# Attention and a gated feed-forward layer in one planned program: due times of the first two units found by trials, scores over 232 keys, and a planned lag before transposes and values

## The chip, the cores and the metric

The kernel runs on one core of one Trainium2 chip. What counts is the device time of one execution in microseconds (us). The engines are TensorE (PE, with its weight loads shown apart as PEld), VectorE (DVE), ScalarE (ACT), GpSimd (POOL) and SyncE (SP, which issues the DMAs here). Each runs its own instructions in a fixed order, and they wait for one another by semaphores.

## What is computed

Sliding-window attention with some global keys, for 4 batches, 8 heads, 768 positions and a head size of 64, and then a gated feed-forward layer over all 3072 tokens (model size 512, inner size 1536). The calls have `n_global` = 8 and `n_local` = 96.

```python
scores = scale * np.matmul(q, k.transpose(0, 1, 3, 2))
is_global = pos[None, :] < int(n_global)
is_local = (rel >= 0) & (rel < int(n_local))
keep = is_global | is_local
dist = np.where(is_global & ~is_local, float(n_local), np.abs(rel))
scores = np.where(keep, scores - slopes * dist, -1000000000.0)
a = softmax(scores)
x = np.matmul(a, v)            # heads side by side: 512 columns per token
out = ((x @ w_a) * (x @ w_b)) @ w_out
```

A query block of 128 positions therefore needs its own 128 keys, the 96 before them and the first 8 of the sequence: 232 keys. The weights arrive as 64-bit floats.

## The kernel before

**Units.** The 24 query blocks (4 batches of 6) are cut into eight units of 4, 2, 3, 3, 3, 3, 3 and 3 blocks (`UNITS`). For a unit, attention makes x, and `moe` runs the feed-forward layer on its tokens in 12 groups `f` of 128 inner columns. Attention of unit u+1 is meant to lie beside the feed-forward layer of unit u; attention of unit 0 (`first`) stands alone at the start. Units 0 and 1 (`PAIRED`) do two heads at once in fp32 (`quad`, scores on L673); units 2 to 7 split q and k into a high and a low fp32r part (`split`) and make each window of scores of two matmuls (`scores` in `attention`, L793).

**Windows.** `Plan` lists for each block which keys it sees. With `G` = 32 and `LW` = 96 a block sees 32 + 96 + 128 = 256 keys. The first block of a batch has 128, and the second shares the first one's keys (joined: 256). `kwin` is the place and width of a block's window of keys, and `vslot` the slots of 128 rows of V that go with it.

**One window.** The scores go to PSUM (`ps`). DVE adds the distance mask and takes the extreme (L537), ACT takes the exponential with its sum (L553), DVE makes the inverse of the sum (L568, L575), ACT or DVE normalises (L585, L587). PE transposes the 128-column pieces (`turn`, L609), ACT or DVE copies them out of PSUM (`pf`, L341 or L343), and PE multiplies them with V (`values`, L626). The mask `rel` and its narrow form `col` are built once, before the first unit (`build_positions`, `build_masks`).

**Feed-forward layer.** For each f, two projections (`p`, L851) of 4 chunks with 3 matmuls each (high and low parts), their product on DVE (L890), its split in two (`hh`, `hl`), and the product with `w_out` into one PSUM bank per block (`acc`, L869). The weights of the 12 groups are converted from 64-bit once, beside unit 0's layer (`load_w`): per half group ACT runs L381 and L418, DVE runs L388, L398, L408, L427 and L351, and one cast (`wt`) runs on ACT (L341) or DVE (L343).

**The order.** Each step is an `Op` with a due time, what it reads and writes, and a cost on each engine that may run it. `Schedule.order` simulates the engines with these costs and with lags between engines (`LAGS`). An engine that comes free takes, among the steps whose inputs are there and whose buffers fit, the one that is due first; `wins` chooses between engines. The order so found is the order in which the instructions are written out. Steps of the first unit have due times before `START` = 52000 (ns), and the layer of unit u is due in equal steps from there.

Of the kernel before, what the change touches and what calls it, by code (L numbers as in the profile page):

```python
# [3 lines left out]

# [8 lines left out]
F32 = mybir.dt.float32  # L13
# [11 lines left out]
P = 128  # L25
# [4 lines left out]
NT = B * S  # L30
G = 32
LW = 96
# [11 lines left out]
SLACK = 1.5  # L44
BACKLOG = 1.0
PRICE = {"dve": 2.0, "pool": 2.0}
TRACE = False
LAGS = {"pe": 200.0, "act": 270.0, "dve": 230.0, "pool": 290.0, "dma": 2300.0}
# [12 lines left out]
class Plan:  # L61
# [4 lines left out]
    def __init__(self, blocks, paired):  # L66
        self.nb = len(blocks)
        self.kkeys = []
        self.vkeys = []
        self.kwin = []  # L70
        self.vslot = []
        self.parts = []
        for n, (b, blk) in enumerate(blocks):
            if blk == 0:
                keys = np.arange(P)
            else:
                q0 = blk * P
                keys = np.concatenate([np.arange(G), np.arange(q0 - LW, q0 + P)])
# [3 lines left out]
            if joined:  # L82
                self.kwin.append((self.kwin[-1][0], 2 * P))
                self.kkeys += [(b, j) for j in keys[P:]]
                self.vslot.append([self.vslot[-1][0], len(self.vkeys)])
                self.vkeys.append((b, keys[P:]))
            else:
                self.kwin.append((len(self.kkeys), len(keys)))
                self.kkeys += [(b, j) for j in keys]
                slots = []  # L90
                for c in range(len(keys) // P):
                    slots.append(len(self.vkeys))
                    self.vkeys.append((b, keys[c * P : (c + 1) * P]))
                self.vslot.append(slots)
        self.nk = len(self.kkeys)
        self.nv = len(self.vkeys)
        self.k0 = self.nb * P
        self.ncol = self.k0 + self.nk // 2
        if paired:

            ends = self.parts[1:] + [self.nk]
            self.pieces = []
            at = 0
            for k, end in zip(self.parts, ends):
                self.pieces.append((at, at + 2 * P - k, 2 * P + end - k, (k, end)))
                at += 2 * P + end - k
            self.ncol = at
# [43 lines left out]
class Op:  # L151
    def __init__(self, index, due, costs, emit, reads, writes, late, port):
        self.index, self.due, self.costs, self.emit, self.late = index, due, costs, emit, late
        self.port = port
        self.bufs, self.after, self.before = [], [], 0
        self.ready, self.engine = 0.0, None
        found = {}
        for is_write, keys in ((False, reads), (True, writes)):
            for key in keys:
                buf, part = key if isinstance(key, tuple) else (key, None)  # L160
                if buf not in self.bufs:
                    self.bufs.append(buf)
                for other, p, w in buf.log:
                    if (w or is_write) and other is not self and (p == part or p is None or part is None):
                        found[other.index] = other
                buf.log.append((self, part, is_write))
        for other in found.values():
            other.after.append(self)
            self.before += 1
        for buf in self.bufs:  # L170
            buf.left += 1


class Schedule:
# [13 lines left out]

    def op(self, due, emit, reads=(), writes=(), late=0.0, port=(), **costs):

        self.ops.append(Op(len(self.ops), due, costs, emit, reads, writes, late, port))

    def order(self):
        free = {e: 0.0 for e in self.SYNC}
# [9 lines left out]
        def arrive(op):  # L204
            for e in op.costs:
                insort(ready[e], (op.due, op.index, op))

# [9 lines left out]
        def wins(op, e):  # L217
            if len(op.costs) == 1:
                return True
            at = {}  # L220
            for o, c in op.costs.items():
                at[o] = max(free[o], now) + c * PRICE.get(o, 1.0)
                for due, index, other in ready[o]:
                    if (due, index) >= (op.due, op.index):
# [5 lines left out]
        for op in self.ops:  # L230
            if not op.before:
                arrive(op)
        while len(out) < len(self.ops):
            started = True
# [31 lines left out]
            if kind == 0:  # L266
                for nxt in op.after:
                    if op.engine == "pe" and tuple(nxt.costs) == ("pe",):
# [37 lines left out]
class Fast:  # L306
# [52 lines left out]
    def load_w(self, f, due):  # L359
# [3 lines left out]
        for g in range(2):  # L363
# [19 lines left out]
                [st],  # L383
                act=act(WN) + 40,
            )
# [36 lines left out]
                [(raw, "lo")],  # L422
                act=act(WN) + 40,
            )
# [105 lines left out]
    def softmax(self, h, due, wins, ps, t, sm):  # L530

        nc, op, n = self.nc, self.plan.op, len(wins)
        for j, (o, w) in enumerate(wins):
            neg = self.negd if w == 2 * P else self.negd0
            op(
# [65 lines left out]

    def turn(self, due, wins, t, pt, pf):

        nc = self.nc
        w = sum(w for o, w in wins)

        def emit(e):
            for c in range(0, w, P):
                nc.tensor.transpose(pt[:, c : c + P], t[:, c : c + P], self.ident)  # L609

        self.plan.op(due, emit, [t], [pt], pe=w / P * 109)
        self.copy(due, lambda: pf[:, :w], lambda: pt[:, :w], w, [pt], [pf], psum=True)

    def values(self, due, pl, blocks, v, probs, pa):
# [20 lines left out]
        n = sum(len(pl.vslot[i]) for i in blocks)  # L635
        self.plan.op(due, emit, reads, [pa], pe=n * 218 + 200)

    def quad(self, u, c, j, due, raw, v, pa, homes):
# [44 lines left out]
        for s in range(2):  # L683
# [11 lines left out]
            self.turn(due, wins, t, pt, pf)  # L695
            for i, (o, w) in zip(blocks, wins):
                probs[s, i] = (pf, o)
        if pa is None:
            pa = self.bank("psS", f"pa{n}")
# [68 lines left out]
    def attention(self, u, start, end):  # L768
# [8 lines left out]
        for c in range(NCC):  # L777
            probs = {}
            v = self.fetch_v(u, c, start + (2 * c + 1) * step - LOADLEAD)
            for s in range(2):  # L780
# [4 lines left out]
                for i in range(pl.nb):  # L785
# [143 lines left out]
    def run(self):  # L929
# [238 lines left out]
def build_positions(nc, cp, tp):  # L1168


    rel = cp.tile([P, 2 * P], F32, name="rel")
    col = cp.tile([P, P], F32, name="col")
    for t, step, base, mult in ((rel, -1, P, 1), (col, 1, 0, 0)):
        nc.gpsimd.iota(
# [5 lines left out]
        )  # L1180
    t = tp.tile([P, 2 * P], F32, name="after")
    nc.vector.tensor_scalar(t, rel, 0.0, BIG, op0=ALU.is_lt, op1=ALU.mult)
    nc.vector.tensor_tensor(rel, rel, t, op=ALU.max)
    return rel, col, t


def build_masks(nc, rel, col, t, nf):

    v, ng, nl = nc.vector, nf[:, 0:1], nf[:, 1:2]
    v.tensor_scalar(t, rel, nl, -BIG, op0=ALU.is_ge, op1=ALU.mult)
    v.tensor_scalar(col, col, ng, -BIG, op0=ALU.is_ge, op1=ALU.mult)
    v.tensor_sub(rel, t, rel)
    v.tensor_scalar(col, col, nl, None, op0=ALU.subtract)
    v.tensor_copy(rel[:, :G], col[:, :G])
    v.tensor_tensor(col, rel[:, P:], col, op=ALU.max)

# [23 lines left out]
def build(nc, a, out):  # L1222
    with tile.TileContext(nc) as tc, ExitStack() as ctx:
        cp = ctx.enter_context(tc.tile_pool(name="c", bufs=1))
        with tc.manual_schedule(), tc.tile_pool(name="tmp", bufs=1) as tp:
# [4 lines left out]
            nc.scalar.activation(spare, lim[:, 0:1], AF.Exp)  # L1230
            rel, col, t = build_positions(nc, cp, tp)
            sc = build_scales(nc, cp)
# [4 lines left out]
            flag = build_flag(nc, cp, nf, lim)  # L1237
            build_masks(nc, rel, col, t, nf)
        fast = nc.values_load(flag[0:1, 0:1], min_val=0, max_val=2**30)
# [12 lines left out]
def pack(q, k, v):  # L1252
# [6 lines left out]
    for u, (blocks, pl) in enumerate(zip(UNITS, PLANS)):  # L1259
# [21 lines left out]
        for c in range(NCC):  # L1281
            vs = [v[b, 2 * c + s, keys] for s in range(2) for b, keys in pl.vkeys]
            put(VOFFS[u][c], np.hstack(vs))
# [32 lines left out]
```

## Time and profile before

| | us |
|---|---|
| median of 3 runs (777.14 to 778.99) | 778.75 |
| the profiled execution | 777.36 |
| its span, first to last instruction | 775.1 |
| PE busy | 751.5 |
| PEld busy | 663.6 |
| DVE busy | 438.7 |
| ACT busy | 433.7 |

PE is busy for 97% of the span, but a matmul's record overlaps the next one's, so a busy PE is not yet a PE at its peak; what a matmul costs in a dense stretch is seen from start to start. DVE and ACT are busy for 57% and 56% of the span on average, and far more at the beginning. The granted TensorE clock was 0.995 of full speed on average.

### The profile page before, as it was taken

Reading aid. Unit: us, or ns where it says so; the run is one execution under the profiler, and the core shown is the slowest. Engines: PE = TensorE matmul, PEld = TensorE weight load, DVE = VectorE, ACT = ScalarE, POOL = GpSimd, SP = SyncE. Lnnn points to the kernel's source line nnn. Section 1 sums busy time; section 2 is a strip of 40 time slices with the busy share of each in tenths; the row PEclk is TensorE's granted clock in tenths of the full one; section 3 lists DMA queues with packets and bytes.
Section 4 is the critical chain, followed back from the end, with each engine's and each line's share of the span. In section 5 each row is a group of like instructions: output and inputs, shape, how many; then the busy total and the mean of one; then the engine's idle time right before and its main releaser. Section 6 shows DMA issues by size and latency. Waiting matters only on the chain.

```text
span 775.1 us, 12558 instructions
## 1 busy us (share of the span) xinstructions
PE 751.5 (97%) x4608; PEld 663.6 (86%) x4608; DVE 438.7 (57%) x1375; ACT 433.7 (56%) x1093; POOL 6.6 (1%) x24
## 2 busy tenths in 40 slices
PE   5799999999999999999999999999999999999997
PEld 4567777798998998989988988999988999889996
DVE  6999999766655654445554554455554545522111
ACT  6999756466656556455555565555544655442111
POOL 1000000000000000000000000000000000000000
PEclk9999999999999999999999999999999999999999
DMA  7888101032221111211112111111112121000001
GB/s 287 334 321 340 35 14 31 32 107 65 75 90 41 62 38 49 72 48 49 43 54 89 42 62 48 48 60 48 52 42 62 62 62 41 0 28 15 1 1 45
DMA packets 20086, 58.04 MB, mean 75 GB/s; under 512 B 2352, under 2 KB 2608, under 8 KB 20016
## 3 DMA queue, kind: packets, MB, share of 16 engines
q1 hardware_dynamic: 20016, 57.16, 21.5%
q8 instruction: 38, 0.62, 0.3%
q14 instruction: 32, 0.26, 0.1%
HBM read 50.86 MB, written 6.29 MB: 74 GB/s over the span
## 4 chain that ended last, share of the span: by engine, by line
PE 84%; DVE 7%; ACT 6%; issue 1%; DMA 1%; ACTq 0%; DVEq 0%
PE p L851 45%; PE acc L869 23%; PE pt L609 5%; PE pa L626 5%; PE ps L793 4%; PE ps L673 1%; ACT wr L418 1%; DVE kk L351 1%; DVE t L537 1%; ACT t L553 1%; ACT t L585 1%; ACT wm L381 1%; DVE wm L408 1%; ACT pf L341 1%; DVE wt L351 1%
## 5 line engine op out<-in xcount | busy, mean ns | idle before, releaser
L851 PE MATMUL p<-xh,wt 128*128 128x384 f32 (+2 forms) x1488 | 438.9, 345 | 4.0 <-DVE wt L343 2.3
L851 PEld LDWEIGHTS p<-xh,wt 128*128 128x128 f32 x1488 | 272.9, 189 | 18.2 <-issue 3.6
L851 PE MATMUL p<-xl,wt 128*128 128x384 f32 (+2 forms) x816 | 269.8, 342 | 0.2 <-DVE xl L351 0.2
L869 PE MATMUL acc<-wt,hh 128*128 128x512 f32 x576 | 206.4, 397 | 0.0
L851 PEld LDWEIGHTS p<-xl,wt 128*128 128x128 f32 x816 | 153.8, 189 | 10.3 <-DVE xl L351 1.4
L890 DVE TENSOR_TENSOR raw<-p,raw 128x384 f32<-128x384 f32 (+2 forms) x96 | 53.4, 557 | 153.5 <-PE p L851 146.8
L869 PEld LDWEIGHTS acc<-wt,hh 128*128 128x128 f32 x576 | 108.3, 188 | 19.0 <-issue 0.5
L553 ACT ACTIVATE t<-t,sm 128x256 f32<-128x256 f32 (+1 forms) x192 | 93.8, 491 | 40.0 <-DVE sm L537 39.0
L869 PE MATMUL acc<-wt,hl 128*128 128x512 f32 x288 | 113.0, 392 | 0.0
L585 ACT ACTIVATE t<-t,sm 128x256 f32<-128x256 f32 (+1 forms) x140 | 68.7, 494 | 71.1 <-DVE sm L575 66.2
L537 DVE CUSTOM_DVE_ANT_0 t<-ps,rel 128x256 f32<-128x256 f32 x160 | 66.6, 421 | 66.9 <-PE ps L793 64.4
L341 ACT COPY raw<-p 128x384 f32<-128x384 f32 (+2 forms) x95 | 45.3, 477 | 70.7 <-PE p L851 70.1
L609 PE MATMUL pt<-ident,t 128*128 128x128 f32 x352 | 68.6, 280 | 5.3 <-ACT t L585 2.5
L341 ACT COPY pf<-pt 128x256 f32<-128x256 f32 (+3 forms) x151 | 56.2, 375 | 22.6 <-PE pt L609 21.6
L351 DVE TENSOR_TENSOR hl<-raw,hh 128x384 fp32r<-128x384 f32 (+2 forms) x96 | 53.4, 556 | 23.7 <-ACT hh L341 23.1
L609 PEld LDWEIGHTS pt<-ident,t 128*128 128x128 f32 x352 | 43.2, 140 | 25.5 <-ACT t L585 10.1
L341 ACT CAST hh<-raw 128x384 fp32r<-128x384 f32 (+2 forms) x85 | 43.6, 513 | 35.9 <-DVE raw L890 34.9
L869 PEld LDWEIGHTS acc<-wt,hl 128*128 128x128 f32 x288 | 54.2, 188 | 6.6
L568 DVE TENSOR_SCALAR sm<-sm 128x1 f32<-128x1 f32 (+1 forms) x168 | 25.7, 153 | 43.5 <-ACT t L553 42.4
L351 DVE TENSOR_TENSOR kk<-raw,kk 64x384 fp32r<-64x384 f32 (+1 forms) x90 | 44.2, 491 | 2.8
L626 PE MATMUL pa<-pf,v 128*64 128x128 f32 x640 | 42.8, 278 | 2.4 <-ACT pf L341 1.9
L626 PEld LDWEIGHTS pa<-pf,v 128*64 128x64 f32 x640 | 34.7, 136 | 11.6 <-issue 5.0
(78 smaller groups left out, 604.7 us busy)
## 6 DMA issues: line engine op xcount, KB each, us to landing
wr<-wts SPq DMA_DIRECT2D x24, 768.0 KB, 12.5
raw<-qkv SPq DMA_DIRECT2D x29, 384.0 KB, 3.0
raw<-qkv SPq DMA_DIRECT2D x24, 320.0 KB, 2.9
v<-qkv SPq DMA_DIRECT2D x16, 384.0 KB, 3.1
out<-o SPq DMA_DIRECT2D x23, 256.0 KB, 2.1
v<-qkv SPq DMA_DIRECT2D x16, 256.0 KB, 2.7
raw<-qkv SPq DMA_DIRECT2D x3, 640.0 KB, 6.0
raw<-qkv SPq DMA_DIRECT2D x1, 256.0 KB, 3.5
```

Source lines behind the costliest of these rows:

```text
L341: self.nc.scalar.copy(out(), src())
L351: lambda e: self.engine(e).tensor_sub(out(), a(), b()),
L537: lambda e, j=j, o=o, w=w, neg=neg: nc.vector.tensor_tensor_reduce(t[:, o : o + w], ps[:, o : o + w], neg[:, :w], -(2.0 ** -(h + 1)), 3.0e ...
L553: lambda e, j=j, o=o, w=w: nc.scalar.activation(t[:, o : o + w], t[:, o : o + w], AF.Exp, bias=sm[:, j : j + 1], scale=-1.0, accum_out=sm[ ...
L568: lambda e: nc.vector.tensor_scalar_add(sm[:, 2 * n : 3 * n], sm[:, n : 2 * n], 1e-9),
L585: nc.scalar.mul(t[:, o : o + w], t[:, o : o + w], r)
L609: nc.tensor.transpose(pt[:, c : c + P], t[:, c : c + P], self.ident)
L626: nc.tensor.matmul(pa[D * s : D * s + D, i * P : i * P + P], v[:, v0 : v0 + D], pf[:, o + c * P : o + c * P + P], start=c == 0, stop=c == ...
L793: nc.tensor.matmul(ps[:, :w], q[:, i * P : i * P + P], kk[:, k0 : k0 + w], start=m == 0, stop=m == 1,)
L851: nc.tensor.matmul(p[:, :T], wt(), b[:, b0 : b0 + T], start=c == 0 and n == 0, stop=c == NCC - 1 and n == 2,)
L869: nc.tensor.matmul(acc[i][:, :], hs[:, i * P : i * P + P], wt(), start=f == 0 and n == 0, stop=f == NF - 1 and n == 2,)
L890: lambda e, asb=asb, pb=pb: nc.vector.tensor_mul(asb[:, :T], pb[:, :T], asb[:, :T]),
```

## The change

**Fewer keys.** `G` goes from 32 to 8, so that a window is 128 + 96 + 8 = 232 keys wide. The order of the keys is turned round: own block, the 96 before, the global ones. The second transpose of a 232 window takes columns 104 to 231; its first 24 columns are there a second time, so the V slot that goes with it has 24 rows of zeros ahead of its 104 keys. The masks are built in the new order, from three index fills in place of two. Joined windows stay at 256 and first blocks at 128.

**A planned lag.** Steps have a field `spare` in place of `late`: the time by which the planner lets a step come later than its input plus the lag. Transposes and values of units 2 to 7 get `SPARE` = 200 ns. The planner's costs change too: transposes 112 ns each in place of 109, values +290 in place of +200, the two ACT steps of the weight conversion +72 in place of +40.

**A search.** `Schedule.search` takes the steps that are due before the end of the second unit's layer, plans them with `order`, and then tries 400 times to move the due time of about 3 in 100 of them at random (normal, 4000 ns). A trial that ends earlier by the model is kept. At last the whole program is planned with the due times so found.

```diff
-G = 32
+G = 8
...
+SPARE = 200.0
...
+TRIES = 400
+SHARE = 0.03
+SPREAD = 4000.0
...
-            joined = blk == 1 and n > 0
...
+            head = np.concatenate([np.arange(P - LW, P), np.arange(P - LW)])
+            if blk == 0:
+                own = np.arange(P, 2 * P) if (b, 1) in blocks else np.arange(0)
+                self.kwin.append((at + len(own), P))
+                self.kkeys += [(b, j) for j in own] + [(b, j) for j in head]
+                self.vslot.append([slot])
+                self.vkeys.append((b, head))
+            elif blk == 1 and n:
+                start, _ = self.kwin[-1]
+                self.kwin.append((start - P, 2 * P))
+                self.vslot.append([slot, self.vslot[-1][0]])
+                self.vkeys.append((b, np.arange(P, 2 * P)))
             else:
...
+                keys = np.concatenate([np.arange(q0, q0 + P), np.arange(q0 - LW, q0), np.arange(G)])
+                self.kwin.append((at, len(keys)))
...
+                self.vkeys += [(b, keys[:P]), (b, keys[P:])]
...
+    def search(self, limit, tries, share, spread):
+        rnd = random.Random(1)
+        ops = [op for op in self.ops if op.due < limit]
+        dues = {op.index: op.due for op in ops}
+        best = self.order(ops, dues)[1]
+        for _ in range(tries):
+            trial = dict(dues)
+            for op in ops:
+                if rnd.random() < share:
+                    trial[op.index] += rnd.gauss(0.0, spread)
+            end = self.order(ops, trial)[1]
+            if end < best:
+                best, dues = end, trial
+        return self.order(self.ops, {op.index: dues.get(op.index, op.due) for op in self.ops})
...
-                        lag = self.SYNC[op.engine] + op.late
+                        lag = self.SYNC[op.engine] + nxt.spare
...
-                act=act(WN) + 40,
+                act=act(WN) + 72,
...
-    def turn(self, due, wins, t, pt, pf):
+    def turn(self, due, wins, t, pt, pf, spare=0.0):
...
+        starts = []
+        for o, w in wins:
+            starts += [o] if w == P else [o, o + w - P]
+        n = len(starts) * P
...
-        self.plan.op(due, emit, [t], [pt], pe=w / P * 109)
-        self.copy(due, lambda: pf[:, :w], lambda: pt[:, :w], w, [pt], [pf], psum=True)
+                nc.tensor.transpose(pt[:, c * P : c * P + P], t[:, o : o + P], self.ident)
+        self.plan.op(due, emit, [t], [pt], pe=len(starts) * 112, spare=spare)
+        self.copy(due, lambda: pf[:, :n], lambda: pt[:, :n], n, [pt], [pf], psum=True)
...
-        self.plan.op(due, emit, reads, [pa], pe=n * 218 + 200)
+        self.plan.op(due, emit, reads, [pa], pe=n * 218 + 290, spare=SPARE if pl.late else 0.0)
...
-                    self.turn(due, [(0, w)], t, pt, pf)
+                    self.turn(due, [(0, w)], t, pt, pf, SPARE)
...
+        t2 = t + NF * (steps[0] + steps[1])
...
-        order, end = self.plan.order()
+        order, end = self.plan.search(t2, TRIES, SHARE, SPREAD)
...
+    for t, base, step, mult in (
+        (rel[:, :P], 0, -1, 1),
+        (rel[:, P:], LW, -1, 1),
+        (first, 0, 1, 0),
+    ):
...
+            vs = [
+                np.vstack([np.zeros((P - len(keys), D), q.dtype), v[b, 2 * c + s, keys]])
+                for s in range(2)
+                for b, keys in pl.vkeys
+            ]
```

More of the change, by code (lines that the diff above doesn't have):

```diff
@@ L3 @@
 from heapq import heappop, heappush
+import random
 import numpy as np
@@ L67, in __init__ @@
         self.nb = len(blocks)
+        self.late = not paired
         self.kkeys = []
@@ L73, in __init__ @@
         for n, (b, blk) in enumerate(blocks):
[L74 to L78, printed above, removed]
-            joined = blk == 1 and n > 0
             if paired and n % 2 == 0:
                 self.parts.append(len(self.kkeys))
[L82 to L86, printed above, removed]
-            else:
-                self.kwin.append((len(self.kkeys), len(keys)))
+            at, slot, q0 = len(self.kkeys), len(self.vkeys), blk * P
+            head = np.concatenate([np.arange(P - LW, P), np.arange(P - LW)])
[10 more added lines that the diff above has]
+                self.vkeys.append((b, np.arange(P, 2 * P)))
+            else:
+                keys = np.concatenate([np.arange(q0, q0 + P), np.arange(q0 - LW, q0), np.arange(G)])
+                self.kwin.append((at, len(keys)))
                 self.kkeys += [(b, j) for j in keys]
[L90 to L94, printed above, removed]
+                self.vslot.append([slot, slot + 1])
+                self.vkeys += [(b, keys[:P]), (b, keys[P:])]
         self.nk = len(self.kkeys)
@@ L151, with __init__ @@
 class Op:
-    def __init__(self, index, due, costs, emit, reads, writes, late, port):
-        self.index, self.due, self.costs, self.emit, self.late = index, due, costs, emit, late
+    def __init__(self, index, due, costs, emit, reads, writes, spare, port):
+        self.index, self.due, self.costs, self.emit, self.spare = index, due, costs, emit, spare
         self.port = port
@@ L171, in __init__, with fresh @@
             buf.left += 1
+        self.found = list(found.values())
+    def fresh(self, due, ops):
+        self.at, self.ready, self.engine = due, 0.0, None
+        self.before = sum(other.index in ops for other in self.found)
+        for buf in self.bufs:
+            buf.left = 0
 class Schedule:
@@ L187, in buf, with op, order @@
         return b
-    def op(self, due, emit, reads=(), writes=(), late=0.0, port=(), **costs):
-        self.ops.append(Op(len(self.ops), due, costs, emit, reads, writes, late, port))
-    def order(self):
+    def op(self, due, emit, reads=(), writes=(), spare=0.0, port=(), **costs):
+        self.ops.append(Op(len(self.ops), due, costs, emit, reads, writes, spare, port))
+    def search(self, limit, tries, share, spread):
[12 more added lines that the diff above has]
+        return self.order(self.ops, {op.index: dues.get(op.index, op.due) for op in self.ops})
+    def order(self, ops, dues):
+        for op in ops:
+            op.fresh(dues[op.index], dues)
+        for op in ops:
+            for buf in op.bufs:
+                buf.left += 1
         free = {e: 0.0 for e in self.SYNC}
@@ L205, in arrive @@
             for e in op.costs:
-                insort(ready[e], (op.due, op.index, op))
+                insort(ready[e], (op.at, op.index, op))
         def fits(op):
@@ L223, in wins @@
                 for due, index, other in ready[o]:
-                    if (due, index) >= (op.due, op.index):
+                    if (due, index) >= (op.at, op.index):
                         break
@@ L228, in wins @@
             return at[e] <= min(at.values()) + 40.0
-        for op in self.ops:
+        for op in ops:
             if not op.before:
                 arrive(op)
-        while len(out) < len(self.ops):
+        while len(out) < len(ops):
             started = True
@@ L267, in order @@
                 for nxt in op.after:
+                    if nxt.index not in dues:
+                        continue
                     if op.engine == "pe" and tuple(nxt.costs) == ("pe",):
@@ L422, in load_w @@
                 [(raw, "lo")],
-                act=act(WN) + 40,
+                act=act(WN) + 72,
             )
@@ L533, in softmax @@
         for j, (o, w) in enumerate(wins):
-            neg = self.negd if w == 2 * P else self.negd0
+            neg = self.negd if w > P else self.negd0
             op(
@@ L600, in softmax @@
             )
-    def turn(self, due, wins, t, pt, pf):
+    def turn(self, due, wins, t, pt, pf, spare=0.0):
         nc = self.nc
-        w = sum(w for o, w in wins)
+        starts = []
+        for o, w in wins:
+            starts += [o] if w == P else [o, o + w - P]
+        n = len(starts) * P
         def emit(e):
-            for c in range(0, w, P):
-                nc.tensor.transpose(pt[:, c : c + P], t[:, c : c + P], self.ident)
-        self.plan.op(due, emit, [t], [pt], pe=w / P * 109)
-        self.copy(due, lambda: pf[:, :w], lambda: pt[:, :w], w, [pt], [pf], psum=True)
+            for c, o in enumerate(starts):
+                nc.tensor.transpose(pt[:, c * P : c * P + P], t[:, o : o + P], self.ident)
+        self.plan.op(due, emit, [t], [pt], pe=len(starts) * 112, spare=spare)
+        self.copy(due, lambda: pf[:, :n], lambda: pt[:, :n], n, [pt], [pf], psum=True)
     def values(self, due, pl, blocks, v, probs, pa):
@@ L695, in quad @@
             self.turn(due, wins, t, pt, pf)
-            for i, (o, w) in zip(blocks, wins):
+            o = 0
+            for i in blocks:
                 probs[s, i] = (pf, o)
+                o += len(pl.vslot[i]) * P
         if pa is None:
@@ L1172, in build_positions @@
     col = cp.tile([P, P], F32, name="col")
-    for t, step, base, mult in ((rel, -1, P, 1), (col, 1, 0, 0)):
+    first = tp.tile([P, P - LW], F32, name="first")
+    for t, base, step, mult in (
[3 more added lines that the diff above has]
+    ):
         nc.gpsimd.iota(
@@ L1180, in build_positions, with build_masks @@
         )
[L1181 to L1187, printed above, removed]
-    v, ng, nl = nc.vector, nf[:, 0:1], nf[:, 1:2]
[L1192 to L1197, printed above, removed]
+    t = tp.tile([P, P + LW], F32, name="after")
+    nc.vector.tensor_scalar(t[:, :P], rel[:, :P], 0.0, BIG, op0=ALU.is_lt, op1=ALU.mult)
+    nc.vector.tensor_tensor(rel[:, :P], rel[:, :P], t[:, :P], op=ALU.max)
+    return rel, col, first, t
+def build_masks(nc, rel, col, first, t, nf):
+    v, ng, nl = nc.vector, nf[:, 0:1], nf[:, 1:2]
+    n = P + LW
+    v.tensor_scalar(t, rel[:, :n], nl, -BIG, op0=ALU.is_ge, op1=ALU.mult)
+    v.tensor_scalar(first, first, ng, -BIG, op0=ALU.is_ge, op1=ALU.mult)
+    v.tensor_sub(rel[:, :n], t, rel[:, :n])
+    v.tensor_scalar(rel[:, n:], first, nl, None, op0=ALU.subtract)
+    v.tensor_copy(col[:, :LW], rel[:, P - LW : P])
+    v.tensor_tensor(col[:, LW:], rel[:, : P - LW], rel[:, n:], op=ALU.max)
 def build_scales(nc, cp):
@@ L1230, in build @@
             nc.scalar.activation(spare, lim[:, 0:1], AF.Exp)
-            rel, col, t = build_positions(nc, cp, tp)
+            rel, col, first, t = build_positions(nc, cp, tp)
             sc = build_scales(nc, cp)
@@ L1237, in build @@
             flag = build_flag(nc, cp, nf, lim)
-            build_masks(nc, rel, col, t, nf)
+            build_masks(nc, rel, col, first, t, nf)
         fast = nc.values_load(flag[0:1, 0:1], min_val=0, max_val=2**30)
@@ L1281, in pack @@
         for c in range(NCC):
-            vs = [v[b, 2 * c + s, keys] for s in range(2) for b, keys in pl.vkeys]
+            vs = [
[3 more added lines that the diff above has]
+            ]
             put(VOFFS[u][c], np.hstack(vs))
```

## The prediction, made before the changed kernel was run

> **What bounds the kernel now.** I read the busy table first (it stands above), then the same table by stages, then the chain of work in order of time, then the waits of TensorE (PE) and the groups of instructions. The stages (length, then busy time of PE, PEld, DVE, ACT, POOL, granted clock, DMA):
>
> ```profile
> 7.60:20.00 12.40, 10.40 (x76) 7.08 (x75) 9.86 (x60) 10.23 (x37) 0.00 (x0) 0.86 1.02 403
> 20.00:32.00 12.00, 10.54 (x102) 7.33 (x100) 10.97 (x63) 12.00 (x43) 0.00 (x0) 1.00 0.95 390
> 32.00:40.00 8.00, 3.28 (x33) 2.22 (x29) 7.42 (x13) 8.00 (x19) 0.00 (x0) 0.97 0.69 261
> 40.00:45.00 5.00, 5.00 (x20) 4.10 (x21) 5.00 (x14) 5.00 (x9) 0.00 (x0) 0.70 0.85 348
> 45.00:80.00 35.00, 34.12 (x174) 26.32 (x174) 34.36 (x62) 34.85 (x58) 0.00 (x0) 1.00 0.77 303
> 80.00:140.00 60.00, 59.62 (x293) 46.87 (x292) 59.29 (x108) 37.58 (x67) 0.00 (x0) 1.00 0.09 25
> ...
> 160.00:700.00 540.00, 537.41 (x3443) 487.52 (x3442) 282.23 (x988) 301.18 (x816) 4.40 (x6) 1.00 0.18 55
> ```
>
> PE is the bound from about 40 us on. From 160 to 700 us it is busy 537.41 of 540, with VectorE (DVE) and ScalarE (ACT) near half. Before 40 us, ACT has no idle time from 20 us on, and DVE hardly any; PE waits for them. From 40 to 140 us PE and DVE are both full: DVE converts the weights while PE uses them, with attention of the second unit as PE's filler. So a gain is to be had in three places: fewer PE cycles anywhere after 40 us, fewer PE stalls after 160 us, and an earlier and smoother first 140 us.
>
> **The change part by part.**
>
> Scores over 232 keys. What a matmul of fp32r costs when PE is dense is read from start to start in the chain (start, length, what, count):
>
> ```profile
> 127.82 5.60 PE p L851 x24
> ...
> 198.38 1.39 PE p L851 x12
> 199.77 0.23 PE ps L793 x2
> ...
> 711.42 4.16 PE p L851 x24
> ...
> 197.58 0.17 PE ps L793 x2
> ```
>
> The L851 rows are 512, 256 and 384 columns wide (the units of four, two and three blocks): 5.60/24 = 233 ns, 1.39/12 = 116 ns, 4.16/24 = 173 ns. That is (173 - 116)/128 = 0.445 ns a column, so 24 columns fewer are 10.7 ns. The scores of the late units follow it: 0.23 us for two of 256 columns. The first block of a batch stays at 128 and the second at 256 (its window joins the first), so per head each batch has four windows of 232. In units 2 to 7 that is 3 x 8 + 9 x 8 = 96 windows of two matmuls: 192 x 10.7 ns = 2.05 us. The pair of 128 columns takes 0.17, not the 0.12 that the slope gives, so something floors narrow matmuls; drawn from 0.17 to 0.23 the slope gives only 96 x 11 ns = 1.1 us. 232 lies next to 256, where the steeper slope holds, so **-2.0 us**, between -1.1 and -2.05. PE is full there, so it counts in full. In the first two units the scores (L673) lie where PE is not alone the bound; I count nothing for them on PE.
>
> Transposes and values keep their number: each 232 window still has two transposes (the second starts at column 104) and two value slots, padded with 24 zero rows, so the copies out of PSUM and the V loads stay as they are. Query/key loads and key splits of the late units get 24 columns a window shorter, on engines half idle: nothing there.
>
> The planned lag. This adds no instruction and no wait: it makes the planner place each transpose and each values step of units 2 to 7 at least 0.2 us after its input, so that other PE work goes first. What it can remove is seen from 160 to 700 us in the waits of PE and of its weight loads:
>
> ```profile
> PE pt L609 <- ACT t L585: 1.9, 7, 0.5
> ...
> PE p L851 <- DVE xl L351: 0.2, 1, 0.2
> ...
> PEld pt L609 <- ACT t L585: 8.8, 23, 0.8
> ```
>
> and in one of these waits, the longest, in the timeline:
>
> ```profile
> 290.32 0.34 PE L851 MATMUL p<-xh,wt 128*128 128x384 f32 x1
> ...
> 291.16 0.20 PEld L609 LDWEIGHTS pt<-ident,t 128*128 128x128 f32 x2 [0.82 <-ACT t L585]
> 291.16 0.44 PE L609 MATMUL pt<-ident,t 128*128 128x128 f32 x2 [0.50 <-ACT t L585]
> ```
>
> A projection matmul starts at 290.32 and another could start 0.173 us later, at 290.49; the transpose starts at 291.16. The stall is 0.67 us. PE's own idle time shows 0.50 of it, because the record of a matmul reaches into the next; the weight loads show 0.82, 0.15 too much. Over 23 waits: 8.8 - 23 x 0.15 = 5.35 us really stalled (estimate). A lag of 0.2 us takes at most 23 x 0.2 = 4.6 us off them, and nothing off what is shorter than that. I take **-3.5 us**; ends 0 (the fixed order meets as many other late inputs) and -5.35. What is queued behind a later transpose: ACT's copy of it, the values, the x copies and the split before the next unit's first projection. That last wait is 0.2 us in all now, and the code ends each attention 1.5 of 12 weight groups early, so 0.2 us a step is covered; if that cover were gone, each of the six unit borders would cost one lag or two, 6 x 0.4 = 2.4 us.
>
> Narrower work in the first 140 us. Per window of 232 instead of 256:
>
> ```profile
> L553 ACT ACTIVATE t<-t,sm 128x256 f32<-128x256 f32 x160 | 81.1, 509 | 35.2 <-DVE sm L537 34.7
> L537 DVE CUSTOM_DVE_ANT_0 t<-ps,rel 128x256 f32<-128x256 f32 x160 | 66.6, 421 | 66.9 <-PE ps L793 64.4 <-PE pt L609 0.8 <-PE ps L673 0.4
> ...
> L587 DVE TENSOR_SCALAR t<-t,sm 128x256 f32<-128x256 f32 x41 | 13.9, 350 | 0.6
> ...
> L553 ACT ACTIVATE t<-t,sm 128x128 f32<-128x128 f32 x32 | 12.8, 401 | 4.8 <-DVE sm L537 4.3
> L537 DVE CUSTOM_DVE_ANT_0 t<-ps,col 128x128 f32<-128x128 f32 x32 | 9.1, 283 | 7.2 <-PE ps L793 5.0 <-PE ps L673 2.2
> ...
> L587 DVE TENSOR_SCALAR t<-t,sm 128x128 f32<-128x128 f32 x11 | 3.1, 284 | 0.2
> ```
>
> DVE: (421 - 283)/128 x 24 = 26 ns, and 12 ns where it normalises, (350 - 284)/128 x 24. ACT: (509 - 401)/128 x 24 = 20 ns. Units 0 and 1 have two such windows each for 8 heads, 32 in all: DVE 32 x 26 + 16 x 12 = 1.0 us, ACT 0.65 us. DVE is full there, so **-0.8 us**, between 0 (if it only makes another hole) and -1.0.
>
> The new mask set-up: three POOL index fills in place of two, and the same six DVE steps on fewer columns. The first score step of DVE waits 1.0 us for PE:
>
> ```profile
> 7.60 0.29 DVE L537 CUSTOM_DVE_ANT_0 t<-ps,col 128x128 f32<-128x128 f32 x1 [1.00 <-PE ps L673]
> ```
>
> This hides it: nothing. Without that cover one more fill would be 0.2 to 0.3 us.
>
> The searched plan. 400 trials change the order of all engines in the first two units, the DMA issues on SP's queue too, and keep what the planner's model says ends first. How much is there? DVE's idle time from 7.6 to 140 us is 2.54 + 1.03 + 0.58 + 0 + 0.64 + 0.71 = 5.5 us by the stage rows; ACT's is 2.17 up to 45 us and 0.15 to 80, but 22.4 from 80 to 140. The DVE work itself does not go: in 40 to 140 us it is mostly
>
> ```profile
> L408 DVE SCALAR_TENSOR_TENSOR wm<-wr,wm 128x768 int32<-128x768 int32 x22 | 20.6, 949 | 0.0
> L427 DVE CUSTOM_DVE_ANT_0 wm<-wr,wm 128x1536 uint16<-128x1536 uint16 x22 | 20.6, 948 | 0.0
> L351 DVE TENSOR_TENSOR wt<-wm,wt 128x768 fp32r<-128x768 f32 x21 | 19.9, 951 | 0.3 <-ACT wt L341 0.3
> L388 DVE TENSOR_SCALAR wm<-wm 128x768 f32<-128x768 f32 x22 | 11.8, 552 | 0.0
> L398 DVE TENSOR_SCALAR wm<-wm 128x768 int32<-128x768 int32 x22 | 11.8, 552 | 0.0
> ```
>
> 84.7 us of weight conversion that only DVE does in this program. Loads are shaken with the rest, and a weight load takes
>
> ```profile
> wr<-wts SPq DMA_DIRECT2D x24, 768.0 KB, 12.5
> ```
>
> from issue to landing (KB, us), with DMA at 0.69 to 1.02 up to 45 us; but no row of ACT's waits names these loads, so a shift by a few us stays covered by their lead. So a perfect order gains about 5.5 us, a useless one 0. Does a gain in the model carry over? The planner's costs against spacings in the chain:
>
> ```profile
> 32.01 0.80 ACT wm L381
> 32.81 0.83 ACT wr L418
> ...
> 36.28 0.87 DVE wm L427
> ```
>
> The ACT conversion is put at 93 + 0.833 x 768 + 72 = 805 ns in the new text (773 before), the DVE step at 67 + 1.045 x 768 = 870 ns: close. I take about a third of 5.5, **-1.7 us**, since every trial keeps a plan fitted to the model alone and lags between engines are single numbers in it. The dearer values (+90 ns) and transposes (+3 ns each) only make the plan place them better; they are within the lag's term.
>
> Sum: -2.0 - 3.5 - 0.8 - 1.7 = -8.0 us. The profiled execution took 777.36 (span 775.1 and 2.3 around it): 769.4. It lies 1.4 under the median of 778.75, which would give 770.75. I predict **770.0**, between them.
>
> **The rivals.**
>
> (All from 778.0, the middle of 777.36 and 778.75.) Only what is certain: the lag moves the stalls elsewhere and the search finds a model's gain alone. For it: 5.35 us of stalls lie in 23 places, and a fixed order can meet 23 others; against it: the close costs above. Scores and narrower windows stay: 778 - 2.8 = 775.2.
>
> The search closes DVE's holes and the lag takes its 4.6: 778 - 2.0 - 4.6 - 1.0 - 5.5 = 764.9. For it: ACT's 22 us of idle time, to which work that either engine can do may move; against it: holes at the start have inputs that are late for everyone.
>
> The clock. After PE's waits of 2.3 and 1.0 us the first projections run slow:
>
> ```profile
> PE p L851 <- DVE wt L343: 2.3, 1, 2.3
> ...
> PE p L851 <- DVE wt L351: 1.0, 1, 1.0
> ...
> 39.87 4.01 PE p L851 x10
> ```
>
> 401 ns each instead of 233, at a granted clock of 0.70 from 40 to 45 us: 10 x 168 ns = 1.7 us. If the new order keeps PE at work before its first projections, this goes on top of the forecast: 768.3. Against it: DVE supplies the weights then, and PE might only wait where it now runs slowly. The Trainium skill, TensorE: Matmul & The Clock Gate, Part 1, says that an idle window of about 3.4 us puts the clock back to half, in windows that run freely; the trace agrees, with 2.3 + 1.0 us of waits ahead of the slow matmuls.
>
> Slower: weight casts go over to DVE. Three of the 24 casts that either engine can do run on DVE now:
>
> ```profile
> L343 DVE CAST wt<-wm 128x768 fp32r<-128x768 f32 x3 | 1.7, 553 | 0.0
> ```
>
> With ACT's conversions priced 32 ns dearer and due times shaken at random, the planner could hand it the other 21: 21 x 0.553 = 11.6 us on the engine that is full from 40 to 140 us. With the scores and the lag kept: 778 - 2.0 - 3.5 + 11.6 = 784.1. It decides from 5.5/0.553, about 10 casts moved on. Against it: the planner counts DVE time double when it chooses.
>
> **How the numbers follow.** A measurement of this kernel tells about 0.3% from no change, 2.3 us: faster means under 776.4, slower over 781.1. Forecast (766 to 773.5) 0.56; only the certain part (773.5 to 777.5) 0.18; holes closed 0.10; clock 0.07; casts on DVE 0.09. Two thirds of the second case lie under 776.4, so faster is 0.56 + 0.12 + 0.10 + 0.07 = 0.85; the rest of it and a third of the last, where few casts move, give same 0.09; slower 0.06. The range from 763.0 to 776.5 leaves out the last case, the worst of the second, and what lies beyond the best.
>
> **What would show it right or wrong.** Now the first projection, and the span of the last weight steps, stand so:
>
> ```profile
> 38.14 0.50 PE L851 MATMUL p<-xh,wt 128*128 128x512 f32 x1 [2.33 <-DVE wt L343]
> ...
> L351 DVE TENSOR_TENSOR wt<-wm,wt x24: 943/951/960, 38.9 to 143.6; 128x768 fp32r<-128x768 f32 x24
> ```
>
> In the changed profile: pairs of L793 at about 0.213 us in the chain and 96 windows of 232; waits of the transposes' weight loads on ACT's normalising from 8.8 down to 4 or 5 us between 160 and 700; DVE's idle time from 7.6 to 140 us down by about 2; the first projection before 38.1 us; clock and weight casts as they were. It is wrong if the stalls come back before other lines, if the last weight conversion still ends near 144 us, or if the casts stand on DVE.

## The result

The changed kernel takes 771.38 us (median of 4 runs, 770.01 to 771.5) beside 778.73 before: a ratio of 0.9905, 95% interval 0.9891 to 0.9919. Its profiled execution took 771.41 us, with a span of 769.6.

The stages of the changed kernel (length, busy time of PE, PEld, DVE, ACT and POOL, granted clock, DMA), cut as those of before:

```profile
7.60:20.00 12.40, 10.42 (x82) 7.25 (x80) 9.73 (x57) 10.62 (x37) 0.00 (x0) 1.00 1.01 405
20.00:32.00 12.00, 9.96 (x90) 6.79 (x86) 11.45 (x63) 12.00 (x43) 0.37 (x1) 1.00 0.94 385
32.00:40.00 8.00, 5.90 (x40) 4.65 (x41) 7.12 (x21) 8.00 (x18) 0.11 (x1) 0.79 0.63 236
40.00:45.00 5.00, 5.00 (x41) 4.05 (x41) 4.55 (x10) 4.56 (x9) 0.00 (x0) 1.00 0.82 306
45.00:80.00 35.00, 33.27 (x159) 26.09 (x158) 34.89 (x63) 34.97 (x58) 0.00 (x0) 1.00 0.80 318
80.00:140.00 60.00, 60.00 (x298) 47.25 (x297) 59.28 (x109) 38.16 (x67) 0.47 (x1) 1.00 0.08 21
160.00:700.00 540.00, 539.39 (x3455) 493.15 (x3454) 274.96 (x983) 301.26 (x822) 2.83 (x4) 1.00 0.17 53
```

Between 40 and 45 us the granted clock is 1.00 in place of 0.70. (The 41 matmuls of PE there and the 20 before don't compare: 22 of the 41 are values and scores of attention, of which before has none in this stretch.) From 160 to 700 us it is busy 539.39 of 540. DVE's idle time from 7.6 to 140 us has hardly changed: 2.67 + 0.55 + 0.88 + 0.45 + 0.11 + 0.72 = 5.4 us (5.5 before).

Its first projection, in the timeline, and its weight conversion, by the view of the tile `wt` (count, shortest, median and longest duration in ns, first and last start in us):

```profile
37.16 0.79 PE L901 MATMUL p<-xh,wt 128*128 128x512 f32 x1
```

```profile
L396 DVE TENSOR_TENSOR wt<-wm,wt x24: 950/954/961, 36.0 to 141.1; 128x768 fp32r<-128x768 f32 x24
L386 ACT CAST wt<-wm x22: 817/840/877, 35.1 to 140.0; 128x768 fp32r<-128x768 f32 x22
L388 DVE CAST wt<-wm x2: 553/554/554, 72.9 to 84.4; 128x768 fp32r<-128x768 f32 x2
```

The first projection comes 1.0 us sooner, the last conversion 2.5 us sooner, and the casts have not gone to DVE. PE's waits between 160 and 700 us have no row any more; the waits of the weight loads ahead of transposes are

```profile
PEld pt L657 <- ACT t L630: 5.4, 20, 0.5
```

(8.8 us in 23 waits before). The chain shows a pair of scores of 232 columns at 0.22 us, where one of 256 took 0.23:

```profile
227.81 0.22 PE ps L843 x2
```

To add the gain up I use the start times of the projection matmuls in the trace: each unit has 288 of them, so the 289th opens unit 1, the 577th unit 2. "Stalls" are the times by which transposes and values after 160 us start later than the dense spacing of the matmul before them allows, where this is over 30 ns. All numbers in the table are us, each from one profile; the ratio is to before on the same chip, with its 95% interval.

| kernel | median | ratio | second weight group | unit 1 | unit 2 | units 2 to 6 | stalls |
|---|---|---|---|---|---|---|---|
| before, first profile | 778.73 | | 50.7 | 156.1 | 225.8 | 466.3 | 5.7 |
| before, again | 778.88 | | 51.0 | 155.8 | 225.6 | 466.6 | 5.6 |
| after, again | 771.3 | 0.9902 (0.9886 to 0.9919) | 49.1 | 153.2 | 221.3 | 464.1 | 1.9 |
| after, old buffer widths | 768.25 | 0.9864 (0.9848 to 0.9881) | 49.3 | 153.4 | 221.2 | 461.9 | 2.1 |
| after, no trials | 778.05 | 0.9992 (0.9983 to 1.0002) | 53.4 | 157.5 | 227.6 | 463.9 | 2.9 |
| 232 keys alone | 778.69 | 0.9992 (0.9982 to 1.0002) | 52.4 | 157.9 | 229.1 | 464.4 | 6.1 |
| 232 keys and new costs | 777.96 | 0.9984 (0.9974 to 0.9993) | 52.7 | 156.8 | 226.7 | 465.8 | 6.1 |
| trials alone | 773.97 | 0.9937 (0.9921 to 0.9954) | 50.7 | 155.8 | 222.7 | 466.4 | 4.0 |

From before to after (the two "again" rows) unit 2 starts 4.2 us sooner, units 2 to 6 take 2.5 us less, and the last unit the same 78.0. That is 6.7 of the 7.65 us by which the span is shorter; the rest lies behind the last matmul, where before took 7.1 us in this profile but 6.0 in its first.

The start of unit 2 does not stand for the same work of PE in all rows. By then PE has done 210 output matmuls (`acc`, 0.23 us each) in most of them, but 216 with the 232 keys alone (1.4 us more) and 207 with the trials alone (0.7 less); and four score matmuls and two transposes more, some 0.6 us, without trials and with keys and new costs. The start of unit 1 can be compared, but for three more output matmuls ahead of it with the trials alone, and so can the start of the last unit (the columns "unit 2" and "units 2 to 6" added): by then PE has done the same number of matmuls of each kind in every row.

### The profile page after: what moved, and what is told of

Same layout as the page of the kernel before. It is cut to its first block, busy times and chain, and to the rows that moved or that the text cites. A ratio compares the mean times of both kernels' runs of the same rounds, so it can differ in the third digit from the quotient of the medians.

```text
span 769.6 us, 12536 instructions
## 1 busy us (share of the span) xinstructions
PE 749.6 (97%) x4608; PEld 666.7 (87%) x4608; DVE 427.7 (56%) x1367; ACT 434.9 (57%) x1101; POOL 5.8 (1%) x25
## 4 chain that ended last, share of the span: by engine, by line
PE 93%; DVE 3%; ACT 3%; issue 0%; DMA 0%; ACTq 0%
PE p L901 51%; PE acc L919 26%; PE pa L674 5%; PE pt L657 5%; PE ps L843 4%; PE ps L721 1%; ACT t L598 1%; DVE kk L396 1%; DVE t L582 1%; ACT wr L463 1%; ACT pf L386 1%; ACT t L630 0%; DMA nv<-ns 0%; DVE ql L550 0%; DVE kk L388 0%
## 5 line engine op out<-in xcount | busy, mean ns | idle before, releaser
L919 PE MATMUL acc<-wt,hh 128*128 128x512 f32 x576 | 208.9, 399 | 0.0
L598 ACT ACTIVATE t<-t,sm 128x232 f32<-128x232 f32 (+2 forms) x192 | 91.4, 478 | 45.0 <-DVE sm L582 43.0
L582 DVE CUSTOM_DVE_ANT_0 t<-ps,rel 128x232 f32<-128x232 f32 (+1 forms) x160 | 63.2, 402 | 87.9 <-PE ps L843 85.9
L630 ACT ACTIVATE t<-t,sm 128x232 f32<-128x232 f32 (+2 forms) x129 | 61.7, 482 | 54.2 <-DVE sm L620 52.7
L396 DVE TENSOR_TENSOR hl<-raw,hh 128x384 fp32r<-128x384 f32 (+2 forms) x96 | 53.4, 556 | 24.3 <-ACT hh L386 24.0
L386 ACT CAST hh<-raw 128x384 fp32r<-128x384 f32 (+2 forms) x91 | 46.7, 513 | 28.9 <-DVE raw L940 28.6
L657 PEld LDWEIGHTS pt<-ident,t 128*128 128x128 f32 x352 | 44.8, 142 | 18.6 <-ACT t L630 7.1
L396 DVE TENSOR_TENSOR kk<-raw,kk 64x348 fp32r<-64x348 f32 (+1 forms) x92 | 42.6, 463 | 2.9
```

What stands on the lines that cost most here:

```text
L386: self.nc.scalar.copy(out(), src())
L396: lambda e: self.engine(e).tensor_sub(out(), a(), b()),
L582: lambda e, j=j, o=o, w=w, neg=neg: nc.vector.tensor_tensor_reduce(t[:, o : o + w], ps[:, o : o + w], neg[:, :w], -(2.0 ** -(h + 1)), 3.0e ...
L598: lambda e, j=j, o=o, w=w: nc.scalar.activation(t[:, o : o + w], t[:, o : o + w], AF.Exp, bias=sm[:, j : j + 1], scale=-1.0, accum_out=sm[ ...
L630: nc.scalar.mul(t[:, o : o + w], t[:, o : o + w], r)
L657: nc.tensor.transpose(pt[:, c * P : c * P + P], t[:, o : o + P], self.ident)
```

## The experiments

All were run with the kernel before beside them on the same chip. The edits are shown against the changed kernel unless said otherwise.

**Both kernels again** (no edit). The last unit holds only the feed-forward layer, which the change doesn't touch, and yet its projections had become slower.

> The kernel before once more, for a profile on the same chip as the runs beside it. In the last unit, where only the feed-forward layer runs, 24 projection matmuls took 4.16 us in the first profile of before and 4.22 us in that of after. If this is the state of a chip or of a run, this profile may show 4.22 too, and the two kernels agree on one chip. If it belongs to the program of after, this one shows 4.16 and after again 4.22.

> The changed kernel once more. Time 0.9905 of before again (771.4). Program theory: the row of 24 projection matmuls in the last unit is 4.22 us, while before shows 4.16. Chip theory: both show the same number.

The chain of work in the last unit, before again and then after again:

```profile
718.00 4.24 PE p L851 x24
722.23 2.07 PE acc L869 x9
```

```profile
704.80 4.23 PE p L901 x24
709.02 2.10 PE acc L919 x9
```

Before shows the slow projections too this time, so the 4.22 is not a mark of the changed program. In after, though, single spacings repeat in fives (173, 175, 175, 181, 176 ns; 176.3 on average from 160 to 690 us) through the whole execution in every profile with its buffer widths, while before again averages 175.2 there, without that pattern. So the next two kernels move the buffers.

**The old widths of two buffers.** `kk` and `raw` are as wide as the widest unit needs, and narrower windows made them narrower; what lies behind them moved.

```diff
-MAXK = max(p.nk for p in PLANS[1:])
+MAXK = 768
-MAXC = max(max(p.ncol for p in PLANS[1:]), 2 * WIDE // 2)
+MAXC = 768
```

> After, with the buffers kk and raw kept as wide as in before (768 columns in place of 696 and 732), so that all later buffers lie where they lay. Layout theory: the slower spacing of the matmuls (176 ns in place of 173.4 for 384 columns) comes from where the operands lie; it goes back to 173.4 and the time falls by some 4 to 5 us, to about 767. Chip or program theory: no difference from after, within 1 us.

```profile
696.18 4.16 PE p L901 x24
700.34 2.06 PE acc L919 x9
```

768.25 us, 3.05 less than after; the two intervals don't meet. The start of unit 2 is as in after, units 2 to 6 take 2.2 us less and the last 1.0. Each engine runs its instructions in the same order in both programs, so the plan makes no difference here. The 1.0 of the last unit can't be laid to the widths: before again, with the old widths, took 78.0 there like after. This version beats both kernels.

**Another place** (`MAXK = 704`, `MAXC = 736`), and **before with a shift** (`MAXC = 772` in before).

> After, with kk 704 and raw 736 columns wide in place of 696 and 732: later buffers move by 768 bytes against before (a multiple of 64), where after moves them by 864 (32 over a multiple of 64). If what counts is the place within 64 bytes: 24 projections in the last unit 4.16 us and about 768.3, as with the old widths. If any other place than the old one is slow: 4.22 and 771.3.

> Before, with raw 772 columns wide in place of 768: later buffers lie 32 bytes further over a multiple of 64, nothing else changes. If the place within 64 bytes counts, the last unit's matmuls of 384 columns take 176 ns with the repeating five (173, 175, 175, 181, 176) that after shows, and the time rises by 1 to 3 us to 780 to 782. If not: 778.9.

The first took 769.71 us (0.9883, 0.9866 to 0.99), between the two, with units 2 to 6 at 462.1 and no pattern of fives, but a last unit at 4.24:

```profile
727.19 4.24 PE p L901 x24
731.43 2.07 PE acc L919 x9
```

The second took 778.65 (0.9995, 0.9985 to 1.0004): no difference, a last unit at 4.18, no fives. So a place within 64 bytes is not the answer; it could not have been, since by the buffer addresses of the built programs the projections' operands (`xh`) start at multiples of 64 in all of these, moved by 832 bytes in after, 768 in the first of these and 64 in the second (the figures in the expectations were mine and wrong). That the widths cost after some 2 to 3 us is shown; what about the place does it is open. Of these programs only after has `xh` at a multiple of 256; no run tests whether that counts.

**No trials.**

```diff
-TRIES = 400
+TRIES = 0
```

> After without the trials (0 in place of 400); keys, lag and costs as in after. My theory (the search is worth 1.7 us): 773.1. Rival, the search only wins in the planner's model: 771.4, no difference. Rival, the search brings most of the gain: 775 or more. The projections of unit 1 start later by what the search is worth.

778.05 us: no difference from before, and 6.75 us over after with the same buffers. The second rival was right: nearly the whole gain needs the search (the other parts together win little more than the new buffer widths, which stand in this kernel too, cost). Almost all of the difference has arisen by the second weight group (53.4 against 49.1 us) and in unit 1 (70.2 against 68.2). What ACT does up to its copy of the first projection, `raw`, which starts at 52.78 us without trials and at 48.43 with them, is in the groups of its instructions up to these times; first without trials, then after again:

```profile
L463 ACT ACTIVATE wr<-wr 128x768 int32<-128x768 uint32 x9 | 8.1, 931 | 0.0
L426 ACT ACTIVATE wm<-wr 128x768 f32<-128x768 f32 x6 | 5.5, 924 | 0.0
L630 ACT ACTIVATE t<-t,sm 128x232 f32<-128x232 f32 (+2 forms) x12 | 5.4, 468 | 0.6 <-DVE sm L620 0.4
L386 ACT CAST wt<-wm 128x768 fp32r<-128x768 f32 x3 | 2.5, 838 | 0.0
```

```profile
L463 ACT ACTIVATE wr<-wr 128x768 int32<-128x768 uint32 x6 | 5.5, 964 | 0.0
L426 ACT ACTIVATE wm<-wr 128x768 f32<-128x768 f32 x5 | 4.7, 940 | 0.0
L630 ACT ACTIVATE t<-t,sm 128x232 f32<-128x232 f32 (+1 forms) x9 | 4.3, 514 | 0.1
L386 ACT CAST wt<-wm 128x768 fp32r<-128x768 f32 x3 | 2.6, 877 | 0.0
```

Without trials ACT also waits once for PE's transposes in the stretch from 30 us on; after has no such row:

```profile
ACT pf L386 <- PE pt L657: 1.1, 1, 1.1
```

Apart from that wait ACT is full there. The wait does not explain the difference: before 30 us, after waits 2.0 us for PE's transposes, where the kernel without trials waits 0.3, so that ACT's idle time from 7.6 us to the copy is about the same, 3.8 us without trials and 3.9 with them. ACT's work explains it. The search moved four conversion steps of later weight groups behind the copy that the first group waits for, 3.5 us from start to start, and ACT does three normalising steps (L630) fewer ahead of it, 0.8: together 4.3 of the 4.35 us. (In unit 1 the kernel without trials has the 0.6 us of extra score matmuls and transposes told above, and 0.6 us of idle time on PE that after has not.) The moved conversion steps cost nothing later, because ACT has over 20 us idle between 80 and 140 us.

**A warm clock without trials.** In the stretch just told the clock differs too. From 40 to 45 us, without trials:

```profile
40.00:45.00 5.00, 5.00 (x14) 4.01 (x15) 5.00 (x12) 3.86 (x7) 0.00 (x0) 0.50 1.01 420
```

Here 12 matmuls that nobody reads (the identity by itself, into a bank that the first projection then overwrites) fill PE's wait for the first weights.

```diff
+                    if u == 0 and f == 0 and which == 0 and c == 0:
+                        for _ in range(12):
+                            nc.tensor.matmul(p[:, :P], self.ident, self.ident, start=True, stop=True)
```

(with `TRIES = 0`)

> After without trials (778.05 us), with 12 throw-away fp32 matmuls of 128 columns put ahead of the first projection, in the 2.8 us in which PE waits for the first weights; the plan does not know of them. The clock theory: without trials the clock is at half speed from 38.2 to 45 us, and 16 projections at 427 ns stand ahead of the transposes on which the last chunk of the first unit waits; kept busy, the clock stays full, the second weight group starts about 2 us earlier (53.4 to 51.4), unit 1 at 155.4 in place of 157.5, and the time is 776. Supply theory: DVE and ACT set that stretch; unit 1 still starts at 157.5 and the time is 778 or a little more.

```profile
37.04 2.94 PE L901 MATMUL p<-ident 128*128 128x128 f32 x24
39.74 0.47 PE L906 MATMUL p<-xh,wt 128*128 128x512 f32 x1
```

```profile
40.00:45.00 5.00, 4.48 (x21) 3.20 (x21) 5.00 (x12) 5.00 (x10) 0.00 (x0) 1.00 1.02 420
```

The clock stayed full and ACT lost no time in this stretch, but PE now waits for ACT instead:

```profile
PE pa L674 <- ACT pf L386: 1.1, 1, 1.1
PE p L906 <- ACT xl L386: 0.9, 1, 0.9
PE p L906 <- ACT raw L386: 0.6, 1, 0.6
```

The second group starts at 53.1 in place of 53.4 and unit 2 at 227.3 in place of 227.6. But this profile is late already before the throw-away matmuls run. ACT's copy of a transpose stands so without them and with them:

```profile
16.30 1.07 ACT L386 COPY pf<-pt 128x512 f32<-128x512 f32 x2 [0.28 <-PE pt L657]
```

```profile
17.48 1.07 ACT L386 COPY pf<-pt 128x512 f32<-128x512 f32 x2 [1.34 <-PE pt L657]
```

From 1.18 us behind, ACT comes to 0.38 ahead at its copy of `raw` (52.40 against 52.78): it wins 1.6 us on the way, most of it the wait of 1.1 for PE that the profile without trials has. The time fell to 776.87 (0.9973, 0.9962 to 0.9985), by 1.2. So neither theory holds as it was put. The cold clock costs some 1.2 to 1.6 us, not nothing, and not the 2 of the clock theory; behind it ACT sets the stretch, as the waits of PE for ACT show.

**232 keys alone, and with the new costs.** Both without trials and lag, with the old widths; the first also takes the planner's costs back.

```diff
-SPARE = 200.0
+SPARE = 0.0
-TRIES = 400
+TRIES = 0
...
-                act=act(WN) + 72,
+                act=act(WN) + 40,
...
-        self.plan.op(due, emit, [t], [pt], pe=len(starts) * 112, spare=spare)
+        self.plan.op(due, emit, [t], [pt], pe=len(starts) * 109, spare=spare)
...
-        self.plan.op(due, emit, reads, [pa], pe=n * 218 + 290, spare=SPARE if pl.late else 0.0)
+        self.plan.op(due, emit, reads, [pa], pe=n * 218 + 200, spare=SPARE if pl.late else 0.0)
```

> After with the 232 keys alone: no trials, no lag, the planner's costs of before, buffers as wide as in before. My step says scores -2.0 and narrower work in the first 140 us -0.8: 776.1 beside 778.9, and the first projection of unit 1 no later than the 155.8 us of before. Rival, the narrower windows upset the hand-set plan of the first units: unit 1 starts later than 156 us, and the time is 778 or more.

> The same with the planner's new costs (conversion +72, values +290, transposes 112), still without trials and lag. If the new costs are what made the untried plan late (unit 1 at 157.5 us without trials, 155.8 before), unit 1 starts 1.5 us or more later than with the 232 keys alone; if not, it starts the same. For the lag: stalls ahead of transposes after 160 us are about 5.6 us in sum again (2 with the lag), and units 2 to 6 take together 3.5 us more than the 461.9 of the kernel with lag and the same buffers. Rival: the stalls stay at 2 us, because the narrower windows or the new costs had removed them.

With the keys alone unit 1 starts at 157.9 us, 2.1 later than before, though every step of the first units got shorter or stayed: my rival of an upset plan. (Unit 2 starts 3.5 later, but 1.4 of that are the six output matmuls done sooner.) The time is that of before, so this loss eats the gain of the scores. The new costs don't make it worse, as one of the expectations had it, but take 1.1 of it back at the start of unit 1 (156.8); by the medians they are worth 0.7. Without the lag, stalls are 6.1 us, and the waits of the weight loads are as in before, or more:

```profile
PEld pt L657 <- ACT t L630: 9.2, 26, 0.5
```

With lag (old widths, with trials) stalls are 2.1 and units 2 to 6 take 461.9 in place of 465.8: 3.9 us, as expected. No two runs differ in the lag alone, though; this pair differs in the trials too. And about 1.4 of the 6.1 us of stalls lie before unit 2.

**Trials alone.** Windows of 256, no lag, old costs, old widths, 400 trials (`G = 32`, `SPARE = 0.0`, the three costs as above).

> Before with the 400 trials alone: windows of 256 keys (in the new order of keys), no lag, the old costs, buffers as wide as in before. If trials find some 5 to 6 us from any start, as they do from the plan with the other parts (227.6 to 221.3 us at the start of unit 2): 773.5, unit 2 at about 220. If they mostly mend what the narrower windows and new costs had spoilt: 777, unit 2 at 224.

773.97 us: the search brings 5 us without any of the other parts; unit 2 starts at 222.7, 2.9 sooner than before, and units 2 to 6 take 466.4 as before. Unit 2 is later than I said (220). The trials do not win here where they won in the plan of after: the second group (50.7) and unit 1 (155.8) start about as in before, and the 2.9 us appear in unit 1. There six output matmuls fewer stand in it (1.4 us; three come sooner, three later), and PE's idle time in it falls from 0.7 us to none. What brought this about in the order was not traced. This profile's span of 772.3 lies 4.9 under that of before again: 2.9 from the start of unit 2, 0.2 from units 2 to 6, 0.9 from the last unit's faster matmuls and 0.9 from behind the last of them. The last two are differences between profiles that the search can't make, so what the plan itself won is about 3 us by the profile and 5 by the medians.

**Another seed** (`random.Random(2)`), and **a lag of 400 ns** (`SPARE = 400.0`), both with the old widths.

> After with the old buffer widths and another seed for the random trials. If the trials reliably find this gain: 768.3, within 1 us. If the first seed was a lucky draw that the planner's model cannot tell from others: 770.5 or more, with a later start of unit 2 than 221.2 us.

> After with the old buffer widths and a lag of 400 ns in place of 200. If the remaining 2.0 us of stalls ahead of transposes after 160 us are of the same kind, they fall under 1 us and units 2 to 6 take 1 us less than 461.9; the total also moves by what the trials find for unit 2's other plan. If longer lags cost elsewhere (values late at the unit borders), units 2 to 6 take more than 461.9.

The seed gives 768.76 (0.9873, 0.9857 to 0.989), with unit 2 at 223.1 and units 2 to 6 at 460.3. Most of that shift is six output matmuls (1.4 us) that this plan does before unit 2 and not after; the last unit starts at 683.4, with the first seed at 683.1. The longer lag gives 767.53 (0.9862, 0.9846 to 0.9879): stalls fall to 0.1 us and the wait of the weight loads for ACT's normalising nearly goes,

```profile
PEld pt L657 <- ACT t L630: 0.3, 2, 0.2
```

and units 2 to 6 take 459.6, 2.3 less than with 200 ns. Here too six output matmuls (1.4 us) come before unit 2; what is left, 0.9, is about the 1 us that was expected. The total can't be told from that with 200 ns (0.9864).

## Why the prediction was right, and where its steps were not

The total of 770.0 was 1.4 us off, by errors that cancel: the search won 3 to 5 us more than forecast, while the narrower work and the buffers' new places lost what the sum didn't have. The nearness is luck; of the mechanisms, the scores and the lag were right.

**Scores.** The mechanism was right, the size was not: a pair takes 219 ns from start to start in the trace, not 213, against 235 before; 96 x 16 = 1.5 us in place of 2.0, between the two ends given.

**Lag.** Right: stalls from 6.1 to 2.1 us, and 3.9 us less in units 2 to 6, where 3.5 was said, with the trials as a second difference. The stalls did not come back elsewhere.

**Narrower work in the first 140 us.** Wrong. I counted shorter steps as time won because DVE is full there. The planner takes at each moment what is due first, so slightly shorter steps gave another order: with the keys alone, unit 1 came 2.1 us later, not 0.8 sooner.

**New costs.** I put them within the lag's term. By themselves they took 1.1 us off the start of unit 1, and 0.7 off the median.

**The search.** Forecast 1.7 us, measured 6.75 (with against without trials) or 5 (alone, by the medians). The step that failed is the one where I bounded it by DVE's idle time of 5.5 us. That idle time is still 5.4. In the plan of after without trials the first unit was held up by the order on ACT, which was full with conversions for later groups ahead of the one copy that the first group waited for, and which had time to spare afterwards. (In the plan of before the trials won elsewhere, in unit 1, and what they mended there is open.) "Full" told me that ACT sets the stretch; it didn't tell me that the work in it had to be there. The doubt that plans which win in the planner's model may not win on the chip was not borne out: the two seeds ended within 0.6 us of each other, by the medians.

**Not in the sum.** The buffers' new places, some 2 to 3 us longer (768.25 to 771.3).

**The rivals.** "Only what is certain" fell with the stalls. The clock did go to full from 40 to 45 us, as that rival had it, and the run with a warm clock puts its price at 1.2 to 1.6 us, near the 1.7 of that rival. It does not come on top of the search, though: the trials themselves made the order in which the clock stays full there, so up to that much of their 6.75 us may be the clock's. Casts on DVE went from 3 to 2.

## What to carry to other kernels

An engine that is full ahead of a late start is not yet a bound: look at which of its steps the start needs, and whether the others could run later, where it has idle time. When an order is made by a planner, each small change of a cost or a width gives a new order; here one such change came 2.1 us later where 0.8 was to be won, so parts must be measured with the same search behind them. A start time compares two orders only where the same work lies ahead of it: count the instructions first. And when sizes of buffers change, compare a stretch that the change doesn't touch.

## What was not expected of the hardware

Dense matmuls with the same shape and a granted clock of 1.00 are not always equally fast: 24 projections of 384 columns took 4.16 us (before, first profile), 4.24 (before again, in its last unit) and 4.22 to 4.23 (after, in both its profiles). In after the spacing repeats in fives, which fits neither the three matmuls of a chunk nor the 24 of a group. The narrower buffers `kk` and `raw` moved the operands by 832 bytes, and the old widths were worth 2 to 3 us; the cause is open. The slow last unit is something else: it appears with the old widths too (before again), and not in every execution.
